# A gated mix of full and local attention: the local branch's sums by accumulating DMAs, padded weights loaded from DRAM

## The chip, the cores and the metric

The kernel runs on one core of a Trainium2 chip. A core has five engines with a queue of instructions each: TensorE (PE) multiplies matrices into the eight banks of PSUM, VectorE (DVE) and ScalarE (ACT) compute on SBUF and PSUM, GpSimd (POOL) and SyncE (SP) mostly issue DMAs here. Engines run side by side and wait for one another through semaphores. The metric is the device time of one execution in microseconds (us), as the median of the runs.

## The reference

Two attentions over 2048 positions of width 640, 32 heads of 20 each, mixed row by row by a sigmoid gate. Both take the input `x`; A attends to all positions, B to the eight positions p, p-2, ..., p-14.

```python
x = A_x
g = _sigmoid((x * gate_w).sum(-1, keepdims=True))
# A: q, k, v from x @ A_wqkv
p = _softmax(einsum("bhqd,bhkd->bhqk", q, k) * scale)
a = merge_heads(einsum("bhqk,bhkd->bhqd", p, v)) @ A_wo
# B: q, k, v from x @ B_wqkv; W, dil = 8, 2
idx = pos[:, None] - (arange(W) * dil)[None, :]
logits = where(idx >= 0, einsum("bhsd,bhswd->bhsw", q, kg) * scale, -1e9)
b = merge_heads(einsum("bhsw,bhswd->bhsd", softmax(logits), vg)) @ B_wo
return g * a + (1 - g) * b
```

`kg` and `vg` are the rows of k and v at the positions `idx`.

## The kernel before

**Branch A.** Queries go in 4 chunks of 512 positions (`qc`), heads in 8 quads of 4 (`q`): 32 groups. A group is 16 key blocks x 4 heads = 64 score matmuls of 32x128 by 32x512. They are cut into steps of 3 and 2 score banks, 819 steps in all. Each step is a set of score matmuls (L956), one exp on ACT over 3 or 2 banks (L969), and the PV matmuls (L977), which collect in one bank; a column of ones in `vA` gives the softmax sums. After a group the bank is transposed by VectorE into `rg` (L586), scaled by gate over sum and transposed back into `oTn` (L594 to L603). The next group's PV matmuls start over in the same bank and wait for L586.

The group's queries are projected just ahead: `cp_w` (L360) copies 80 weight columns from `WqkA` into a padded tile `WqP` with 32 columns a head (20 used, the first of them for a bound on the scores), five matmuls (L378) project, VectorE evacuates twice (`qtmp` L537, `qT` L545). In the first chunk the keys of each quad are made in the same way through `WkP` (`gen_k`). `WqkA` holds all q and k weights of branch A: two small loads for quad 0 at the start on ACT's queue, two of 700 KB on SP's.

**Branch B** runs beside it, one chunk of 512 positions at a time. Stage F (`gen_F`) projects q and k, multiplies them at the eight offsets (L739) and sums over the head with matmuls. Stage K (`gen_K`) projects v into `vB4`, makes the softmax over eight offsets, and for each of four blocks of 128 positions spreads the weights to `attnT` (eight PE transposes, one evacuation L830) and sums `vB4` x weight over the eight offsets on VectorE: the first product goes to `blkacc` (L847), each further one to `tmpB` (L853) and is added (L857), the last add goes to `oBacc` as bf16 (L863).

**Output.** `gen_fold` adds both branches' output projections per block and half width: 5 matmuls of B and 8 of A (13), evacuation, a store. For the last chunk `gen_prefold` does 5 of B and 6 of A (11) for eight pieces, 88 matmuls, and keeps them in `accin`; `last_fold`, behind the last exp, does the last two quads (16 matmuls, L665), adds (L672) and stores. The prefold needs stage K of the last chunk complete.

**The order** of each engine's queue is written out by a planner in Python when the program is built. It walks through the 819 steps, keeps a model clock for each engine, and lets "lanes" (generators such as `gen_F`, `gen_K`, `gen_fold`, the k, q and v projections) add instructions between the steps. A lane yields `("dve", need, weight)` or `("pe", need, weight)` and goes on when the model clock has room; `after(t)` holds it until task `t` is done by the model; a lane has a window of steps and goes on when it is behind its share. What a step needs and isn't there is forced (`force`), which takes no regard of room or waits. Lanes that are unfinished after step 819 are forced then, in order. The model charges each DMA 4000 ns from the moment at which its inputs are ready, and each engine instruction its `cost`. Banks 6 and 7 are handed to the lanes by `take` and `give`.

Dependencies come from keys: a task waits for the writers of what it reads, and for writers and readers of what it writes. A DMA's completion is always a semaphore wait, also between two DMAs of one queue. All engines take their queue in order. DMA semaphores rotate, 16 on SP and 12 on POOL.

Of the kernel before, what the change touches and what calls it, by code (L numbers as in the profile page):

```python
# [5 lines left out]
FP32 = mybir.dt.float32  # L6
# [3 lines left out]
ALU = mybir.AluOpType  # L10
# [208 lines left out]
def _build(ctx, nc, A_x, A_wqkv, A_wo, B_wqkv, B_wo, gate_w, out):  # L219
# [21 lines left out]
    bw = sb([P, 3328], BF16, "bw")  # L241
# [49 lines left out]
    lgt = [WqkA[:, 2 + i, D:D + 512] for i in range(2)]  # L291
    repp = [[WqkA[:, 0, D:D + 512], WqkA[:, 1, D:D + 512]], [WkP[i][:, 0:4, :].rearrange("p c k -> p (c k)") for i in range(2)]]
    rep_dead = [[("WkA", 1)], [("WkP", 0), ("WkP", 1)]]
    accin = WqkB[:, :, :].rearrange("p c k -> p (c k)").bitcast(FP32)[:, 0:4 * D].rearrange("p (b k) -> p b k", b=4)
    outl = WvB[:, :, :].rearrange("p c k -> p (c k)")[:, 0:4 * D].rearrange("p (b k) -> p b k", b=4)

# [7 lines left out]
        return bass.AP(tensor=t, offset=first.offset, ap=[[first.ap[0][0], P]] + dims)  # L304


    T("act", lambda e: e.dma_start(WqkA[:, :, D:D + 80], wA_v[:, :, D:D + 80]), writes=[("WkA", 0)], dma=True)
# [8 lines left out]

    T("act", sp_gw, writes=["gw"], dma=True)
    T("sp", lambda e: e.dma_start(WvA[:, :, 2:D + 2], wA_v[:, :, 2 * D:3 * D]), writes=["WvA"], dma=True)
    T("sp", lambda e: e.dma_start(WqkA[:, :, D + 80:2 * D], wA_v[:, :, D + 80:2 * D]), writes=[("WkA", 1)], dma=True)
    T("sp", lambda e: e.dma_start(WqkA[:, :, 80:D], wA_v[:, :, 80:D]), writes=[("WqA", 1)], dma=True)  # L320

    T("pool", lambda e: e.iota(itmp, [[1, P]], base=0, channel_multiplier=-1), writes=["itmp"])
    T("pool", lambda e: e.iota(stmp, [[P, CN], [-DH, 32]], base=0, channel_multiplier=1), writes=["stmp"])
# [16 lines left out]
        T("dve", lambda e, j=j: e.memset(e0[32 * j:32 * j + 1, :], 1.0), writes=["e0"])  # L340
        T("dve", lambda e, j=j: e.memset(nsel[32 * j:32 * j + 32, 32 * j:32 * j + 1], -1.0), writes=["nsel"])
    for i in range(2):
        T("dve", lambda e, i=i: e.memset(WkP[i][:, :, :], 0.0), writes=[("WkP", i)])
        T("dve", lambda e, i=i: e.memset(WqP[i][:, :, :], 0.0), writes=[("WqP", i)])
# [11 lines left out]

    def cp_w(dst, src_first):
        o_ap = fap(dst, dst[:, 0, 1:2], [[P, CN], [32, 4], [1, DH]])
        i_ap = fap(WqkA, src_first, [[2 * D, CN], [DH, 4], [1, DH]])
        return lambda e: e.tensor_copy(o_ap, i_ap)  # L360

    wk_made = set()

    def mk_wk(q):
        wk_made.add(q)
        return T("dve", cp_w(WkP[q % 2], WqkA[:, 0, D + 80 * q:D + 80 * q + 1]),
                 reads=[("WkA", 0 if q == 0 else 1)], writes=[("WkP", q % 2)], cost=370)

    def mk_wq(q, i):
        return T("dve", cp_w(WqP[i], WqkA[:, 0, 80 * q:80 * q + 1]),  # L370
                 reads=[("WqA", 0 if q == 0 else 1)], writes=[("WqP", i)], cost=370)

    def mm_part(b, mms, k0, n, reads, cost):

# [56 lines left out]
    def after(t):  # L431
        return ("t", t.fin)
# [88 lines left out]

    def gen_q(gi):
        qc, q = divmod(gi, NQUAD)
        i = gi % 2
        yield ("dve", 370.0, 0.0)
        yield after(mk_wq(q, i))
        while qc == 0 and not kl[q].done:
            yield ("poll",)
        b = yield from take()
        yield from chain(b, proj_mms(b, WqP[i], qc), [("WqP", i), "xT"])  # L530
# [155 lines left out]
    sm_b = fap(sm, sm[:, 0, 0:1], [[32, 4], [0, WIN], [1, 32]])  # L686
    prodctr = [0]
    fdone, ldone = {}, {}

    def gen_F(tc):  # L690

# [14 lines left out]
                yield ("dve", 690.0, 0.0)  # L706
                give(b, T("dve", lambda e, dst=dst, b=b: e.tensor_copy(dst, bank[b]), reads=[("bk", b)], writes=[key], cost=690))  # L707
        while tc > 0 and not ldone.get(tc - 1):
            yield ("poll",)
        while (NQUAD - 1) not in wk_made:  # L710
            yield ("poll",)
        for half in range(2):
            b = yield from take()
            slot = {}

            def sel(f, b=b, slot=slot):
                rs = [slot[(f, wp)] for wp in range(4)]

                def pe_l(e):
                    ins = None  # L720
                    for wp in range(4):
                        ins = e.matmul(bank[b][32 * wp:32 * wp + 32, :], Sel[:, f, :], prod[rs[wp]][:, :],  # L722
                                       start=(f == 0), stop=(f == CN - 1))
# [24 lines left out]
            yield ("dve", 690.0, 0.0)  # L748
            give(b, T("dve", lambda e, half=half, b=b: e.tensor_copy(lgt[half], bank[b]),
                      reads=[("bk", b)], writes=[("lgt", half), ("WkA", 1)], cost=690))  # L750
        if tc == 0:
            for w in range(1, WIN):
                row = 32 * (w % 4)
# [4 lines left out]
    def gen_K(tc):  # L758
# [77 lines left out]
        mk_aT(0, b)  # L836
        yield ("dve", 690.0, 690.0)
        give(b, ev_aT(0, b))
        for bl in range(4):
            ai = bl % 2  # L840
            for w in range(WIN):
                av = fap(bw, attnT[ai][:, w * P:w * P + 1], [[0, CN], [1, P]])
                off = PADB - DIL * w + bl * P
                vv = vB4[:, :, off:off + P]
                yield ("dve", 822.0, 822.0)
                if w == 0:
                    T("dve", lambda e, vv=vv, av=av: e.tensor_tensor(blkacc[:, :, :], vv, av, ALU.mult),  # L847
                      reads=[("aT", ai), "vB4"], writes=["blkacc"], cost=822)
# [4 lines left out]
                T("dve", lambda e, vv=vv, av=av: e.tensor_tensor(tmpB, vv, av, ALU.mult),  # L853
                  reads=[("aT", ai), "vB4"], writes=["tmpB"], cost=822)
                yield ("dve", 822.0, 822.0)
                if w < WIN - 1:
                    T("dve", lambda e: e.tensor_tensor(blkacc[:, :, :], blkacc[:, :, :], tmpB, ALU.add),  # L857
                      reads=["tmpB"], writes=["blkacc"], cost=822)
                else:
                    while tc >= 1 and not folddone.get(tc - 1):  # L860
                        yield ("poll",)
                    acc = oBacc[:, :, bl * P:(bl + 1) * P]
                    T("dve", lambda e, acc=acc: e.tensor_tensor(acc, blkacc[:, :, :], tmpB, ALU.add),  # L863
                      reads=["tmpB", "blkacc"], writes=[("oBacc", bl)], cost=822)
                if w == 3 and bl < 3:
                    yield after(tr)
                    b = yield from take()
# [8 lines left out]
    mk_wk(0)  # L876

    def pro_tr(t):
        bs = (0, 1, 2) if t % 2 == 0 else (3, 4, 5)
# [21 lines left out]

    def pro_k(t):
        b = 6 + t % 2
        mm_part(b, proj_mms(b, WkP[0], t), 0, CN, [("WkP", 0)] + [("xTt", t, k) for k in range(3)], 1100)
        k_evac(b, 0, t, "act")

    pro_tr(0)
    pro_tr(1)
    mk_wq(0, 0)
    pro_k(0)  # L910
    pro_tr(2)
    pro_k(1)
    consts_late()
    pro_tr(3)
    QB0 = 0
    mm_part(QB0, proj_mms(QB0, WqP[0], 0), 0, CN, [("WqP", 0)] + [("xTt", 0, k) for k in range(3)], 1100)
# [4 lines left out]
    pro_k(3)  # L921
    sch.bufs["xT"] = sch.bufs[("xTt", 3, 2)]
    mk_KM(0)
    for gi_ in range(2):
# [284 lines left out]
```

## Time and profile before

| | us |
|---|---|
| median of 2 runs | 1102.41 |
| the runs | 1106.39, 1098.44 |
| span of the profiled execution (its own full time is not among the runs) | 1091.2 |
| first exp starts, last exp ends | 27.8, 1080.3 |
| VectorE busy in the span | 579.7 |
| mean granted TensorE clock | 0.831 of full speed |

The span is the time from the first to the last instruction in one profiled execution. Further groups that the change touches, each with line, engine, operation, tiles, count, then busy us and mean ns of one:

```profile
L863 DVE TENSOR_TENSOR oBacc<-blkacc,bw 128x640 bf16<-128x640 f32 x16 | 13.2, 824 | 0.5
L360 DVE COPY WqP<-WqkA 128x400 bf16<-128x400 bf16 x32 | 11.6, 364 | 0.2 <-DMA WqkA<-in_A_wqkv_dram 0.2
L653 DVE COPY WqkB<-ps 128x320 f32<-128x320 f32 x8 | 3.9, 491 | 24.1 <-PE ps L378 24.1
```

The number behind the second bar is the engine's idle time just before these instructions, with what ended it. POOL is busy for 0.7 us in the whole span, and no DMA is issued from it.

### The profile page before, as it was taken

The page shows a single profiled execution, that of the slowest core. Times are in us where ns is not written, and L with a number is a line of the kernel's source. Part 1 is how long each engine was busy: PE and PEld are TensorE (multiplying, and loading weights), DVE is VectorE, ACT ScalarE, POOL GpSimd, SP SyncE. Part 2 cuts the span into 40 slices and gives each one's busy share as a digit, 9 for nine tenths or more (in the row PEclk, how much of TensorE's full clock was granted, in tenths as well). Part 3 has the DMA queues.
Part 4 walks back from the last instruction along what each step waited for, and adds up shares of the span by engine and source line. Part 5 has one row for each costly group of instructions (what it writes and reads, how often), then busy time and mean ns, then how long its engine had stood idle before and what let it go on. Part 6 is the DMA issues. An engine that isn't in the chain of part 4 may idle for free.

```text
span 1091.2 us, 15504 instructions
## 1 busy us (share of the span) xinstructions
PE 969.2 (89%) x5820; PEld 289.7 (27%) x5894; DVE 579.7 (53%) x1055; ACT 971.4 (89%) x842; POOL 0.7 (0%) x6
## 2 busy tenths in 40 slices
PE   6978899998798898989998988998888899799997
PEld 3323333322222222123332122233222223222231
DVE  4355434443635755762467767225787723777512
ACT  4868889988999988989999989999998989898996
POOL 0000000000000000000000000000000000000000
PEclk9879989998999756689998677999976699755695
DMA  8000000000000000000000000000000000000000
GB/s 277 1 1 15 17 1 2 1 23 9 1 2 1 1 1 1 1 1 7 7 7 7 1 1 1 7 8 7 7 2 1 1 7 13 7 1 1 1 1 25
DMA packets 11356, 12.79 MB, mean 12 GB/s; under 512 B 2708, under 2 KB 10644, under 8 KB 11284
## 3 DMA queue, kind: packets, MB, share of 16 engines
q1 hardware_dynamic: 9028, 11.27, 3.2%
q8 instruction: 49, 0.80, 0.3%
q10 hardware_dynamic: 2256, 0.53, 0.2%
q14 instruction: 23, 0.19, 0.1%
HBM read 9.18 MB, written 2.62 MB: 11 GB/s over the span
## 4 chain that ended last, share of the span: by engine, by line
PE 63%; ACT 21%; issue 9%; DVE 6%; DMA 1%; ACTq 0%; SPq 0%; DVEq 0%
ACT ebuf L969 21%; PE ps L956 20%; PE ps L378 19%; PE ps L977 19%; PE ps L453 2%; PE ps L543 1%; DVE bw L853 1%; PE ps L722 1%; DMA x_tm<-in_A_x_dram 1%; DVE blkacc L857 1%; PE ps L823 1%; DVE rg L586 1%; DVE qT L545 1%; DVE qtmp L537 0%; DVE WvB L672 0%
## 5 line engine op out<-in xcount | busy, mean ns | idle before, releaser
L969 ACT ACTIVATE ebuf<-ps 128x1536 bf16<-128x1536 f32 (+1 forms) x819 | 956.0, 1245 | 84.9 <-PE ps L956 64.3
L956 PE MATMUL ps<-qT,kT 32*128 32x512 bf16 x2048 | 372.9, 448 | 87.7 <-ACT ebuf L969 69.8
L977 PE MATMUL ps<-ebuf,vA 128*21 128x512 bf16 x2048 | 373.8, 452 | 3.3 <-DVE rg L586 1.2
L956 PEld LDWEIGHTS ps<-qT,kT 32*128 32x128 bf16 x2048 | 87.3, 93 | 370.5 <-PE ps L956 153.2
L977 PEld LDWEIGHTS ps<-ebuf,vA 128*21 128x21 bf16 x2048 | 77.7, 90 | 239.3 <-issue 229.7
L853 DVE TENSOR_TENSOR bw<-vB,bw 128x640 f32<-128x640 bf16 x112 | 91.9, 820 | 2.2
L857 DVE TENSOR_TENSOR blkacc<-blkacc,bw 128x640 f32<-128x640 f32 x96 | 79.0, 823 | 2.8
L739 DVE TENSOR_TENSOR prod<-qk 128x512 bf16<-128x512 bf16 x160 | 57.7, 418 | 22.3 <-PE ps L722 22.1
L707 DVE CAST qk<-ps 128x512 bf16<-128x512 f32 x40 | 27.6, 689 | 75.3 <-PE ps L378 72.6
L378 PE MATMUL ps<-xT,WqkB 128*128 128x512 bf16 x181 | 63.0, 413 | 3.2 <-issue 1.8
L537 DVE CAST qtmp<-ps 128x512 bf16<-128x512 f32 x32 | 22.1, 691 | 76.3 <-PE ps L378 73.6
L586 DVE STREAM_TRANSPOSE rg<-ps 128x512 f32<-128x512 f32 x32 | 22.9, 716 | 69.2 <-PE ps L977 69.2
L378 PE MATMUL ps<-xT,WqP 128*128 128x512 bf16 x134 | 52.1, 457 | 4.0 <-issue 1.8
L378 PE MATMUL ps<-woA_r,oTn 128*128 128x320 bf16 x240 | 54.2, 303 | 0.1
L390 DVE TENSOR_SCALAR kT<-ps,e 128x512 bf16<-128x512 f32 x28 | 20.9, 746 | 61.8 <-PE ps L378 60.0
L378 PE MATMUL ps<-xT,WkP 128*128 128x512 bf16 x145 | 48.8, 407 | 2.1 <-issue 1.0
L378 PE MATMUL ps<-WvA,oBacc 128*128 128x320 bf16 x160 | 38.0, 310 | 0.9 <-issue 0.4
L771 DVE CAST vB<-ps 128x512 bf16<-128x512 f32 x20 | 13.7, 687 | 46.5 <-PE ps L378 42.6
L633 DVE CAST outsb<-ps 128x320 bf16<-128x320 f32 x24 | 11.7, 488 | 44.7 <-PE ps L378 44.5
L545 DVE CAST qT<-ps 128x512 bf16<-128x512 f32 x32 | 22.1, 692 | 23.8 <-PE ps L543 22.6
L453 PE MATMUL ps<-WvA,xT 128*128 128x160 bf16 (+1 forms) x320 | 32.6, 244 | 1.5 <-DVE WvA L919 1.0
L378 PE MATMUL ps<-xT,WvB 128*128 128x512 bf16 x88 | 28.8, 389 | 0.8 <-DVE vB L771 0.4
(90 smaller groups left out, 448.4 us busy)
## 6 DMA issues: line engine op xcount, KB each, us to landing
x_tm<-in_A_x_dram SPq DMA_DIRECT2D x4, 640.0 KB
out_dram<-outsb SPq DMA_DIRECT2D x12, 160.0 KB
WqkB<-in_B_wqkv_dram SPq DMA_DIRECT2D x1, 1600.0 KB
WqkA<-in_A_wqkv_dram SPq DMA_DIRECT2D x2, 700.0 KB
WvA<-in_A_wqkv_dram SPq DMA_DIRECT2D x1, 800.0 KB
qk<-in_B_wqkv_dram SPq DMA_DIRECT2D x1, 800.0 KB
woA_r<-in_A_wo_dram SPq DMA_DIRECT2D x32, 25.0 KB
WvA<-in_B_wo_dram SPq DMA_DIRECT2D x5, 160.0 KB
```

The lines of the kernel that those rows point to most:

```text
L378: ins = e.matmul(o, l, r, start=(k0 + k == 0), stop=(k0 + k == n - 1))
L453: ins = e.matmul(bank[b][:, i_ * wn:(i_ + 1) * wn], xT[:, c, kb * P:(kb + 1) * P], WvA[:, c, w0:w0 + wn], start=(c == 0), stop=(c == CN - 1))
L537: T("dve", lambda e: e.tensor_copy(qtmp[:, :], bank[b]), reads=[("bk", b)], writes=["qtmp"], cost=690)
L545: return T("dve", lambda e: e.tensor_copy(qT[gi % NQT][:, :], bank[b]), reads=[("bk", b)], writes=[("qT", gi % NQT)], cost=690)
L586: return T("dve", lambda e: e.transpose(rg[i][:, :], bank[OB]), reads=[("ob", j) for j in range(4)], writes=[("rg", i)], cost=720)
L707: give(b, T("dve", lambda e, dst=dst, b=b: e.tensor_copy(dst, bank[b]), reads=[("bk", b)], writes=[key], cost=690))
L739: t = T("dve", lambda e, r=r, f=f, off=off: e.tensor_tensor(prod[r][:, :], qB[:, f, :], kB[:, f, off:off + 512], ALU.mult), reads=["qB", " ...
L853: T("dve", lambda e, vv=vv, av=av: e.tensor_tensor(tmpB, vv, av, ALU.mult), reads=[("aT", ai), "vB4"], writes=["tmpB"], cost=822)
L857: T("dve", lambda e: e.tensor_tensor(blkacc[:, :, :], blkacc[:, :, :], tmpB, ALU.add), reads=["tmpB"], writes=["blkacc"], cost=822)
L956: ins = e.matmul(bank[b0 + i], kT[32 * j:32 * j + 32, q, kb * P:(kb + 1) * P], qT[gi % NQT][32 * j:32 * j + 32, :], start=True, stop=True)
L969: return T("act", lambda e: e.activation(ebuf[s % NEB][:, 0:512 * n], ps[:, b0 * 512:(b0 + n) * 512], ACTF.Exp, scale=SCALE), reads=[("bk" ...
L977: ins = e.matmul(bank[OB][32 * j:32 * j + DH + 1, :], vA[:, q, kb, VW * j:VW * j + DH + 1], ebuf[s % NEB][:, i * 512:(i + 1) * 512], start ...
```

## The change

1. The running sum of a block of stage K. Products go as fp32 into a ring of three tiles `tmps`; for each, GpSimd's queue issues a DMA that adds the tile to `accs[ac]`, one of two accumulators that alternate by block. The first product of a block is written to `accs` directly. A block is closed by a copy from `accs` to `oBacc`, one block later (`close`). A product waits in the plan until the DMA that read its tile is done by the model.
2. `WqkA` shrinks to 160 columns, the weights of quad 0. All others are loaded by SP straight into `WkP` and `WqP`, five DMAs for a weight, one for each 128 rows, in runs of 20 elements; the weight of quad q+2 (or group gi+2) is issued when the projection with the tile's present content has been recorded. The copies L360 stay for quad 0 alone.
3. `lgt` and `repp`, which lay in dead columns of `WqkA`, get a tile of their own, `lgtr`; the wait of `gen_F` for the last `WkP` is gone.

```diff
-    tmpB = bw[:, 2048:2048 + 2 * D].bitcast(FP32).rearrange("p (c k) -> p c k", c=CN)
-    WqkA = sb([P, CN, 2 * D], BF16, "WqkA")
+    WqkA = sb([P, CN, 160], BF16, "WqkA")
+    lgtr = sb([P, 4, 512], BF16, "lgtr")
-    blkacc = sb([P, CN, P], FP32, "blkacc")
+    NTM = 3
+    tmps = [sb([P, D], FP32, "tmps%d" % i) for i in range(NTM)]
+    accs = [sb([P, D], FP32, "accs%d" % i) for i in range(2)]
...
-    T("sp", lambda e: e.dma_start(WqkA[:, :, D + 80:2 * D], wA_v[:, :, D + 80:2 * D]), writes=[("WkA", 1)], dma=True)
-    T("sp", lambda e: e.dma_start(WqkA[:, :, 80:D], wA_v[:, :, 80:D]), writes=[("WqA", 1)], dma=True)
...
+    def ld_w(dst, key, col):
+        for c in range(CN):
+            o_ap = fap(dst, dst[:, c, 1:2], [[32, 4], [1, DH]])
+            i_ap = bass.AP(tensor=A_wqkv.tensor, offset=A_wqkv.offset + c * P * 3 * D + col, ap=[[3 * D, P], [DH, 4], [1, DH]])
...
+            T("sp", fn, writes=[(key[0], key[1], c)], dma=True)
...
     def gen_k(q):
-        yield ("dve", 370.0, 0.0)
-        yield after(mk_wk(q))
         for tcc in range(4):
             b = yield from take()
-            yield from chain(b, proj_mms(b, WkP[q % 2], tcc), [("WkP", q % 2), "xT"])
+            yield from chain(b, proj_mms(b, WkP[q % 2], tcc), w_keys("WkP", q % 2) + ["xT"])
+            if tcc == 3 and q + 2 < NQUAD:
+                ld_wk(q + 2)
...
     def gen_q(gi):
-        yield ("dve", 370.0, 0.0)
-        yield after(mk_wq(q, i))
...
+        yield from chain(b, proj_mms(b, WqP[i], qc), w_keys("WqP", i) + ["xT"])
+        if gi + 2 < QCN * NQUAD:
+            ld_wq(gi + 2)
...
+        def close(bl):
+            ac, r, t = blkq.pop(0)[1:]
+            yield after(t)
+            yield ("dve", 822.0, 822.0)
+            while tc >= 1 and not folddone.get(tc - 1):
+                yield ("poll",)
+            acc = oBacc[:, :, bl * P:(bl + 1) * P]
+            T("dve", lambda e: e.tensor_copy(acc, acc3[ac]), reads=[("accs", ac)], writes=[("oBacc", bl)], cost=420)
...
-                T("dve", lambda e, vv=vv, av=av: e.tensor_tensor(tmpB, vv, av, ALU.mult),
-                  reads=[("aT", ai), "vB4"], writes=["tmpB"], cost=822)
-                yield ("dve", 822.0, 822.0)
...
+                r = tmctr[0] % NTM
+                tmctr[0] += 1
+                rd_ = tmrd.get(r)
+                if rd_ is not None:
+                    yield after(rd_)
+                    yield ("dve", 822.0, 0.0)
+                T("dve", lambda e, vv=vv, av=av, r=r: e.tensor_tensor(tmp3[r], vv, av, ALU.mult),
+                  reads=[("aT", ai), "vB4"], writes=[("tmps", r)], cost=822)
+                t = T("pool", lambda e, r=r, ac=ac: e.dma_start(accs[ac][:, :], tmps[r][:, :], accum_op=ALU.add),
+                      reads=[("tmps", r)], writes=[("accs", ac)], dma=True)
+                tmrd[r] = t
+                if w == 1 and blkq:
+                    yield from close(bl - 1)
+                if w == WIN - 1:
+                    blkq.append((bl, ac, r, t))
...
+        yield from close(3)
         bdone[tc] = True
```

More of the change, by code (lines that the diff above doesn't have):

```diff
@@ L240, in _build @@
     vB4 = sb([P, CN, 512 + PADB], BF16, "vB4")
-    bw = sb([P, 3328], BF16, "bw")
+    bw = sb([P, 2048], BF16, "bw")
     attnT = [bw[:, 1024 * i:1024 * i + 1024] for i in range(2)]
-    tmpB = bw[:, 2048:2048 + 2 * D].bitcast(FP32).rearrange("p (c k) -> p c k", c=CN)
     NPR = 6
@@ L288, in _build @@
     oBacc = sb([P, CN, 512], BF16, "oBacc")
-    blkacc = sb([P, CN, P], FP32, "blkacc")
-    lgt = [WqkA[:, 2 + i, D:D + 512] for i in range(2)]
-    repp = [[WqkA[:, 0, D:D + 512], WqkA[:, 1, D:D + 512]], [WkP[i][:, 0:4, :].rearrange("p c k -> p (c k)") for i in range(2)]]
-    rep_dead = [[("WkA", 1)], [("WkP", 0), ("WkP", 1)]]
+    NTM = 3
+    tmps = [sb([P, D], FP32, "tmps%d" % i) for i in range(NTM)]
+    accs = [sb([P, D], FP32, "accs%d" % i) for i in range(2)]
+    tmp3 = [t[:, :].rearrange("p (c k) -> p c k", c=CN) for t in tmps]
+    acc3 = [t[:, :].rearrange("p (c k) -> p c k", c=CN) for t in accs]
+    lgt = [lgtr[:, 2 + i, :] for i in range(2)]
+    repp = [[lgtr[:, 0, :], lgtr[:, 1, :]], [WkP[i][:, 0:4, :].rearrange("p c k -> p (c k)") for i in range(2)]]
+    rep_dead = [[], [("WkP", i, c) for i in range(2) for c in range(CN)]]
     accin = WqkB[:, :, :].rearrange("p c k -> p (c k)").bitcast(FP32)[:, 0:4 * D].rearrange("p (b k) -> p b k", b=4)
@@ L304, in fap @@
         return bass.AP(tensor=t, offset=first.offset, ap=[[first.ap[0][0], P]] + dims)
-    T("act", lambda e: e.dma_start(WqkA[:, :, D:D + 80], wA_v[:, :, D:D + 80]), writes=[("WkA", 0)], dma=True)
+    T("act", lambda e: e.dma_start(WqkA[:, :, 80:160], wA_v[:, :, D:D + 80]), writes=[("WkA", 0)], dma=True)
     for t in range(QCN):
@@ L342, in _build @@
     for i in range(2):
-        T("dve", lambda e, i=i: e.memset(WkP[i][:, :, :], 0.0), writes=[("WkP", i)])
-        T("dve", lambda e, i=i: e.memset(WqP[i][:, :, :], 0.0), writes=[("WqP", i)])
+        T("dve", lambda e, i=i: e.memset(WkP[i][:, :, :], 0.0), writes=[("WkP", i, c) for c in range(CN)])
+        T("dve", lambda e, i=i: e.memset(WqP[i][:, :, :], 0.0), writes=[("WqP", i, c) for c in range(CN)])
     def consts_late():
@@ L358, in cp_w, with mk_w0, fn, ld_wk @@
         o_ap = fap(dst, dst[:, 0, 1:2], [[P, CN], [32, 4], [1, DH]])
-        i_ap = fap(WqkA, src_first, [[2 * D, CN], [DH, 4], [1, DH]])
+        i_ap = fap(WqkA, src_first, [[160, CN], [DH, 4], [1, DH]])
         return lambda e: e.tensor_copy(o_ap, i_ap)
[L362 to L371, printed above, removed]
+    def mk_w0(dst, key, c0, src):
+        return T("dve", cp_w(dst, WqkA[:, 0, c0:c0 + 1]), reads=[src], writes=[key], cost=370)
+    def ld_w(dst, key, col):
+        for c in range(CN):
+            o_ap = fap(dst, dst[:, c, 1:2], [[32, 4], [1, DH]])
+            i_ap = bass.AP(tensor=A_wqkv.tensor, offset=A_wqkv.offset + c * P * 3 * D + col, ap=[[3 * D, P], [DH, 4], [1, DH]])
+            def fn(e, o_ap=o_ap, i_ap=i_ap):
+                with nc.allow_non_contiguous_dma(reason="runs of one head"):
+                    return e.dma_start(o_ap, i_ap)
+            T("sp", fn, writes=[(key[0], key[1], c)], dma=True)
+    def ld_wk(q):
+        ld_w(WkP[q % 2], ("WkP", q % 2), D + 80 * q)
+    def ld_wq(gi):
+        ld_w(WqP[gi % 2], ("WqP", gi % 2), 80 * (gi % NQUAD))
+    def w_keys(name, i):
+        return [(name, i, c) for c in range(CN)]
     def mm_part(b, mms, k0, n, reads, cost):
@@ L529, in gen_q @@
         b = yield from take()
-        yield from chain(b, proj_mms(b, WqP[i], qc), [("WqP", i), "xT"])
+        yield from chain(b, proj_mms(b, WqP[i], qc), w_keys("WqP", i) + ["xT"])
+        if gi + 2 < QCN * NQUAD:
+            ld_wq(gi + 2)
         yield ("dve", 690.0, 0.0)
@@ L688, in _build @@
     fdone, ldone = {}, {}
+    tmctr = [0]
+    tmrd = {}
     def gen_F(tc):
@@ L708, in gen_F @@
         while tc > 0 and not ldone.get(tc - 1):
-            yield ("poll",)
-        while (NQUAD - 1) not in wk_made:
             yield ("poll",)
@@ L749, in gen_F @@
             give(b, T("dve", lambda e, half=half, b=b: e.tensor_copy(lgt[half], bank[b]),
-                      reads=[("bk", b)], writes=[("lgt", half), ("WkA", 1)], cost=690))
+                      reads=[("bk", b)], writes=[("lgt", half)], cost=690))
         if tc == 0:
@@ L838, in gen_K @@
         give(b, ev_aT(0, b))
+        blkq = []
+        def close(bl):
[6 more added lines that the diff above has]
+            T("dve", lambda e: e.tensor_copy(acc, acc3[ac]), reads=[("accs", ac)], writes=[("oBacc", bl)], cost=420)
         for bl in range(4):
             ai = bl % 2
+            ac = bl % 2
             for w in range(WIN):
@@ L846, in gen_K @@
                 if w == 0:
-                    T("dve", lambda e, vv=vv, av=av: e.tensor_tensor(blkacc[:, :, :], vv, av, ALU.mult),
-                      reads=[("aT", ai), "vB4"], writes=["blkacc"], cost=822)
+                    T("dve", lambda e, vv=vv, av=av, ac=ac: e.tensor_tensor(acc3[ac], vv, av, ALU.mult),
+                      reads=[("aT", ai), "vB4"], writes=[("accs", ac)], cost=822)
                     if bl < 3:
@@ L852, in gen_K @@
                     continue
-                T("dve", lambda e, vv=vv, av=av: e.tensor_tensor(tmpB, vv, av, ALU.mult),
-                  reads=[("aT", ai), "vB4"], writes=["tmpB"], cost=822)
-                yield ("dve", 822.0, 822.0)
[L856 to L864, printed above, removed]
+                r = tmctr[0] % NTM
[13 more added lines that the diff above has]
+                    blkq.append((bl, ac, r, t))
                 if w == 3 and bl < 3:
@@ L872, in gen_K, with mk_k0, mk_q0 @@
                     give(b, ev_aT(bl + 1, b))
+        yield from close(3)
         bdone[tc] = True
-    mk_wk(0)
+    def mk_k0():
+        mk_w0(WkP[0], ("WkP", 0, 0), 80, ("WkA", 0))
+        for c in range(1, CN):
+            sch.bufs[("WkP", 0, c)] = [sch.bufs[("WkP", 0, 0)][0], []]
+    def mk_q0():
+        mk_w0(WqP[0], ("WqP", 0, 0), 0, ("WqA", 0))
+        for c in range(1, CN):
+            sch.bufs[("WqP", 0, c)] = [sch.bufs[("WqP", 0, 0)][0], []]
+    mk_k0()
     def pro_tr(t):
@@ L903, in pro_k @@
         b = 6 + t % 2
-        mm_part(b, proj_mms(b, WkP[0], t), 0, CN, [("WkP", 0)] + [("xTt", t, k) for k in range(3)], 1100)
+        mm_part(b, proj_mms(b, WkP[0], t), 0, CN, w_keys("WkP", 0) + [("xTt", t, k) for k in range(3)], 1100)
         k_evac(b, 0, t, "act")
@@ L908, in _build @@
     pro_tr(1)
-    mk_wq(0, 0)
+    mk_q0()
+    ld_wk(1)
+    ld_wq(1)
     pro_k(0)
@@ L915, in _build @@
     QB0 = 0
-    mm_part(QB0, proj_mms(QB0, WqP[0], 0), 0, CN, [("WqP", 0)] + [("xTt", 0, k) for k in range(3)], 1100)
+    mm_part(QB0, proj_mms(QB0, WqP[0], 0), 0, CN, w_keys("WqP", 0) + [("xTt", 0, k) for k in range(3)], 1100)
     pro_k(2)
@@ L921, in _build @@
     pro_k(3)
+    ld_wk(2)
+    ld_wq(2)
     sch.bufs["xT"] = sch.bufs[("xTt", 3, 2)]
```

## The prediction

> **What bounds the kernel now.** I read the page first: busy time, chain, groups.
>
> ```profile
> span 1091.2 us, 15504 instructions
> ...
> PE 969.2 (89%) x5820; PEld 289.7 (27%) x5894; DVE 579.7 (53%) x1055; ACT 971.4 (89%) x842; POOL 0.7 (0%) x6
> ...
> PE 63%; ACT 21%; issue 9%; DVE 6%; DMA 1%; ACTq 0%; SPq 0%; DVEq 0%
> ...
> L969 ACT ACTIVATE ebuf<-ps 128x1536 bf16<-128x1536 f32 (+1 forms) x819 | 956.0, 1245 | 84.9 <-PE ps L956 64.3
> ...
> L853 DVE TENSOR_TENSOR bw<-vB,bw 128x640 f32<-128x640 bf16 x112 | 91.9, 820 | 2.2
> L857 DVE TENSOR_TENSOR blkacc<-blkacc,bw 128x640 f32<-128x640 f32 x96 | 79.0, 823 | 2.8
> ```
>
> PE and ACT carry the kernel: 819 exps, 956.0 us of work in the 1052.5 us between the first exp (27.8 us) and the end of the last (1080.3). VectorE is on 6% of the chain. Its adds (L857) are the work the change takes off it, so I asked who waits for them:
>
> ```profile
> who waited for it (us, times):
>   PEld ps L378: 2.6, 5
>   PE ps L956: 0.5, 1
>   PEld ps L823: 0.4, 1
>   PE ps L378: 0.3, 1
> ```
>
> That is 3.8 us for 79.0 us of work; the same view gives 1.9 us for the products L853 and 1.8 us for the weight copies L360. So 7.5 us at most comes back directly. Then the stages at the end, busy us of PE, PEld, DVE, ACT, POOL, then the granted clock:
>
> ```profile
> 1022.00:1058.00 36.00, 35.18 (x232) 12.13 (x230) 9.19 (x18) 32.88 (x28) 0.00 (x0) 0.95 0.00 1
> 1058.00:1080.30 22.30, 19.66 (x102) 4.36 (x99) 0.49 (x1) 22.20 (x20) 0.00 (x0) 0.62 0.00 1
> 1080.30:1091.20 10.90, 4.22 (x19) 1.87 (x19) 6.29 (x13) 0.00 (x0) 0.00 (x0) 0.66 0.18 61
> ```
>
> In the first, the prefold of the last chunk (88 matmuls) runs under the exps; only 10.9 us lie behind the last exp. The change attacks exactly this.
>
> **What the change moves.** Removed from VectorE: 96 adds at 0.82 us (79.0), 16 closing adds (13.2) and 38 of 40 weight copies (0.36 each, 14). Added: 16 closing copies (between the 0.36 us of an L360 copy of 400 elements and the 0.82 of a closing add). The 112 adds become accumulating DMAs on GpSimd's queue. Each writes the accumulator that the previous one of its block wrote, so each waits for the previous landing; products go into a ring of three buffers, so product n waits, at the head of VectorE's in-order queue, for accumulate n-3. Behind it stand the evacuations of banks 6 and 7, the group's `rg` transpose (the next group's PV matmuls wait for it) and `qT`.
>
> The planner charges 4 us to a DMA and holds a product back until its buffer should be free. This stretches the local branch's stage K. In the changed program's recorded order, the steps (exps) from first to last accumulate are 253-350, 423-527 and 631-713 for chunks 0 to 2. Chunk 3 begins at step 777 of 819 and isn't done at the last step. What is left is written out behind the last exp: PE's order ends with the last block's 8 transposes, all 88 prefold matmuls and the 16 of the last fold; VectorE's has, behind the last group's norm, 13 more products, three `oBacc` copies, 8 prefold evacuations and 8 final adds. Cover for that work is gone.
>
> **Price of one accumulate (L).** The trace has no accumulating and no GpSimd DMA. The nearest rows are chains on SP's queue, each DMA waiting for the one before (total us, times, longest):
>
> ```profile
> SPq L570 <- DMA woA_r<-in_A_wo_dram: 29.3, 24, 1.3
> SPq L578 <- DMA WvA<-in_B_wo_dram: 14.7, 4, 3.7
> ```
>
> Waiting plus issue gives 1.2 + 0.3 = 1.5 us for a 25 KB load and 3.7 + 0.5 = 4.2 us for a 160 KB load in 128 rows of 1280 B. A final output store of 160 KB lands 1.8 us after issue. An accumulate moves 320 KB in 128 rows of 2560 B and has to read the destination too. Bounds: 1.8 us (faster than its bytes suggest) and 6.9 us (4.2 with the 2.7 us above the small load doubled for twice the bytes). I take 4.2, the nearest chained row of 128 rows. By the Trainium skill (DMA: Bandwidth & Descriptors, Anatomy of one DMA) a GpSimd DMA costs about 2.0 us plus bytes/436 GB/s, an estimate of 2.75 us here; the sum would be +46 us, 1148. No run here shows it yet; the 4.2 us row speaks for more.
>
> **The tail.** Accumulates of a block are serial; the first of a block can run beside the last of the block before. So four blocks take 7 + 6 + 6 + 6 = 25 L, at 4.2 us 105 us. From step 777 to the last exp are 42 steps; the last undisturbed stretch gives 1.167 us a step (29.2 us between the norms at 1051.8 and 1081.0, 25 steps), 49 us. So 105 - 49 = 56 us of chain lie behind the last exp. At small L the order sets a floor: about 4 us to the norm's end and the next product, then 12 L.
>
> Then come the closing copy (0.8) and the first prefold evacuation (0.5). Two of eight prefold pieces wait in their banks; the other 66 matmuls need banks back. The last fold shows their price at both clocks:
>
> ```profile
> 1080.85 2.32 PE L665 MATMUL ps<-woA_r,oTn 128*128 128x320 bf16 x8
> ...
> 1083.51 1.37 PE L665 MATMUL ps<-woA_r,oTn 128*128 128x320 bf16 x8 [0.34 <-DVE oTn L603]
> 1083.96 4.66 DVE L672 TENSOR_TENSOR WvB<-ps,WqkB 128x320 bf16<-128x320 f32 x8 [0.51 <-PE ps L665]
> ```
>
> 0.29 or 0.17 us each, 19 or 11 us; I take 15. Evacuations (0.49) hide beside them. The last fold's first eight: 1.8 (1.4 to 2.3). From its second eight to the end as now: 1091.2 - 1083.5 = 7.7. Sum behind the last exp: 56 + 0.8 + 0.5 + 15 + 1.8 + 7.7 = 82 us, where 10.9 stand now: **+71**.
>
> **The body.** Back come the 7.5 us of waits and, with the prefold gone from 1022-1058, 36.0 - 32.9 = 3.1 us down to ACT's busy time: -11. Against it stand the weights. SP now issues 190 loads of 20 KB in runs of 40 B for two of 700 KB, and branch B's weights (2.4 MB, 9 us at the 277 GB/s of the first slice) are queued behind the k weights of group 3, which wait for a projection at about step 22; their reader stands at step 32, some 13 us later. I take +5 us (0 to 10) for this and late weights. The ring costs nothing at 4.2 us: at 1.286 us a step ((1080.3 - 27.8)/819) the tightest places of chunk 2's order (product 7 at step 649, behind five serial accumulates: 18 x 1.286/5) stall only from L = 4.6 to 4.8 us on. Body -6; sum +71 - 6 = +65 on the profiled execution. Its own span is 1091.2; the median is 11.2 us longer for launch and spread between runs, which I carry over: 1102.4 + 65 = **1167**.
>
> **Rivals.**
> *The ring stalls the body* (L above 4.8). For: two reads and a write per byte, queue and descriptors on GpSimd. Against: planned spacing above 4.2. At L = 5.4: tail 135 - 49 = 86 of chain, 30 more than above; chunks need 135 us where they have 125, 134 and 105 (97, 104 and 82 steps): 10 + 1 + 30. Together 1167 + 71 = 1238. At 6.9 it is 1167 + 67 + 152 = 1386. Copies of VectorE that hold up accumulates would lead here, and the skill has such a rule (SBUF - State Buffer, SBUF: two separate sides): GpSimd can't write descriptors while VectorE runs a two-port copy. No row here shows it. Chance 0.28.
> *Short accumulates.* At 1.8 us: floor 4 + 21.6 = 26 of chain instead of 56, 1137; with body gains twice as large 1126. For: a 160 KB store lands in 1.8. Chance 0.09.
> *Faster: the body becomes ACT-bound.* Place: steps 253 to 777. All 96 us in which exps don't run would vanish because VectorE is 106 us freer: +71 - 96 = -25, 1077. It decides from a body gain of 93 us on; from 49 on it is no measurable change. For: DVE 0.6 busy in these stages. Against: 7.5 us of waits. Chance 0.03 with the cases between.
> *Weights late.* A 160 B-run load of 640 pieces took 6.8 us to land at the busy start; five loads of 512 pieces, if serial, are 34 us, more than a group of 29. If seven k groups each wait 5 to 10 us: +35 to +70, 1202 to 1237. Against: loads are queued without waiting for one another and one group ahead. Chance 0.05.
>
> **Numbers.** Forecast (L from 3 to 4.8: 1151 to 1182) 0.55; rivals 0.28, 0.09, 0.03, 0.05. Range 1142 to 1240: below it lie most of the short accumulates, 0.07, above it half of the ring's cases, 0.13. Two per cent (22 us) is about what a measurement here tells from no change. Faster 0.01; same 0.04, the short accumulates with more body gain and most of the ACT-bound cases; slower 0.95.
>
> **What would show it.** In the changed profile: a last exp near 1075, then 60 to 100 us with ACT empty; VectorE waiting for DMA at the products; accumulates about 4.2 us apart there; 66 matmuls in 11 to 19 us behind them. The ring rival shows `tmps` products waiting for DMA between 350 and 950 us with ACT idle; late weights show PE waiting for `WkP` or `WqP`. I am wrong if ACT is busy to the end, or if accumulates land in under 1.5 us.

## The result and the profile after

The changed kernel takes 1156.21 us (two runs, 1154.84 and 1157.59) against 1102.41: 1.049 times as long, with an interval of 1.043 to 1.056. That is +53.8 us between the medians, where +65 was forecast. The page of the changed kernel, with the rows that answer to those of before:

```profile
span 1152.9 us, 15953 instructions
...
PE 987.2 (86%) x5823; PEld 295.6 (26%) x5894; DVE 488.0 (42%) x921; ACT 971.2 (84%) x842; POOL 97.3 (8%) x118
...
q0 software_dynamic: 16128, 36.71, 17.2%
...
PE 59%; ACT 23%; issue 12%; DVE 4%; DMA 2%; POOL 1%; ACTq 0%; SPq 0%; DVEq 0%; POOLq 0%
...
L1013 ACT ACTIVATE ebuf<-ps 128x1536 bf16<-128x1536 f32 (+1 forms) x819 | 955.9, 1243 | 82.7 <-PE ps L1000 62.2
...
L887 POOL DMA_DIRECT2D accs<-tmps x112 | 96.7, 889 | 1030.3 <-DVE tmps L885 773.1
```

VectorE is busy 92 us less (579.7 to 488.0). ACT does the same 956 us of exps, and PE does the same matmuls (5820 and 5823 records, 969.2 and 987.2 us). So no work was added to the two engines that carry the kernel, and the span is still 61.7 us longer. The stages say where; again busy us of PE, PEld, VectorE, ACT and POOL, then the granted clock, for the last stretch before the end of the last exp (1077.9 us) and for what lies behind it:

```profile
1000.00:1077.90 77.90, 69.79 (x400) 19.26 (x400) 35.50 (x55) 74.69 (x65) 11.79 (x15) 0.72 0.31 60
1077.90:1152.90 75.00, 20.36 (x115) 12.38 (x115) 23.99 (x39) 0.01 (x1) 12.36 (x15) 0.61 0.37 74
```

Up to the last exp nothing is slower: ACT is busy for 74.7 of the 77.9 us, and the last exp ends 2.4 us earlier than before (1077.9 against 1080.3). Behind it ACT is empty for 75.0 us where 10.9 stood: +64.1 - 2.4 = +61.7, the whole of the difference. What fills the first 53 of these 75 us is the queue of GpSimd; its timeline there (start, us, instruction, idle time before and what ended it):

```profile
1083.39 0.86 POOL L887 DMA_DIRECT2D accs<-tmps  x1 [4.33 <-DVE tmps L885]
1087.19 0.86 POOL L887 DMA_DIRECT2D accs<-tmps  x1 [2.95 <-DMA accs<-tmps]
1090.99 0.86 POOL L887 DMA_DIRECT2D accs<-tmps  x1 [2.94 <-DMA accs<-tmps]
1094.78 0.86 POOL L887 DMA_DIRECT2D accs<-tmps  x1 [2.93 <-DMA accs<-tmps]
1098.56 0.86 POOL L887 DMA_DIRECT2D accs<-tmps  x1 [2.92 <-DMA accs<-tmps]
1102.36 1.75 POOL L887 DMA_DIRECT2D accs<-tmps  x2 [2.94 <-DMA accs<-tmps]
1107.99 0.86 POOL L887 DMA_DIRECT2D accs<-tmps  x1 [3.88 <-DMA accs<-tmps]
```

Each start is about 3.8 us after the last one: 0.86 to issue, 2.94 of waiting for the landing. That is L. At 1102.36 two go out together, the last of one block and the first of the next. The queue goes on like this to 1127.47, and that accumulate has landed at 1131.0, when VectorE and PE take over. The timeline of all engines at the two ends of the prefold:

```profile
1131.01 0.82 DVE L862 CAST oBacc<-accs 128x640 bf16<-128x640 f32 x1 [11.05 <-DMA accs<-tmps]
...
1132.37 1.49 PE L392 MATMUL ps<-WvA,oBacc 128*128 128x320 bf16 x5 [44.96 <-DVE WqkB L667]
...
1143.32 2.56 PE L679 MATMUL ps<-woA_r,oTn 128*128 128x320 bf16 x16
```

PE has stood idle for 45 us for one VectorE copy (L667) that frees a bank. This copy stands in VectorE's queue behind the closing copy of the last block (L862), and so behind all the accumulates. Then PE runs the 66 prefold matmuls in 1143.32 - 1132.37 = 10.95 us, and the last fold with its output takes the 9.6 us to the end.

The span grew by 61.7 us and the median by 53.8 because the profiled execution of before was near the short end: its span is 1091.2, while 54 later runs of the same kernel took 1092.2 to 1107.7, with medians of 1097.8, 1103.4 and 1098.3 on the three chips used below. Between span and time lie only 1.9 us (1152.9 and 1154.84).

### The profile page after: what moved, and what is told of

Its sections match the earlier page's. It is cut to its first block, busy times and chain, and to the rows that moved or that the text cites. A ratio compares the mean times of both kernels' runs of the same rounds, so it can differ in the third digit from the quotient of the medians.

```text
span 1152.9 us, 15953 instructions
## 1 busy us (share of the span) xinstructions
PE 987.2 (86%) x5823; PEld 295.6 (26%) x5894; DVE 488.0 (42%) x921; ACT 971.2 (84%) x842; POOL 97.3 (8%) x118
## 4 chain that ended last, share of the span: by engine, by line
PE 59%; ACT 23%; issue 12%; DVE 4%; DMA 2%; POOL 1%; ACTq 0%; SPq 0%; DVEq 0%; POOLq 0%
ACT ebuf L1013 22%; PE ps L1000 19%; PE ps L1021 18%; PE ps L392 17%; PE ps L467 2%; DMA accs<-tmps 1%; PE ps L837 1%; PE ps L736 1%; POOL accs L887 1%; DMA x_tm<-in_A_x_dram 1%; DVE rg L600 1%; PE ps L557 0%; DVE WvB L686 0%; DVE mx L806 0%; DVE L_sb L808 0%
## 5 line engine op out<-in xcount | busy, mean ns | idle before, releaser
L1013 ACT ACTIVATE ebuf<-ps 128x1536 bf16<-128x1536 f32 (+1 forms) x819 | 955.9, 1243 | 82.7 <-PE ps L1000 62.2
L1000 PE MATMUL ps<-qT,kT 32*128 32x512 bf16 x2048 | 381.4, 458 | 83.5 <-ACT ebuf L1013 66.5
L1021 PE MATMUL ps<-ebuf,vA 128*21 128x512 bf16 x2048 | 380.5, 461 | 4.3 <-DVE rg L600 2.0
L887 POOL DMA_DIRECT2D accs<-tmps x112 | 96.7, 889 | 1030.3 <-DVE tmps L885 773.1
L1000 PEld LDWEIGHTS ps<-qT,kT 32*128 32x128 bf16 x2048 | 87.7, 94 | 371.5 <-PE ps L1000 163.4
L885 DVE TENSOR_TENSOR tmps<-vB,bw 128x640 f32<-128x640 bf16 x112 | 89.2, 818 | 77.3 <-DMA accs<-tmps 77.1
L392 PE MATMUL ps<-xT,WqP 128*128 128x512 bf16 x135 | 55.0, 481 | 6.5 <-ACT ebuf L1013 3.0
L392 PE MATMUL ps<-xT,WqkB 128*128 128x512 bf16 x186 | 58.1, 390 | 1.4 <-issue 0.7
L392 PE MATMUL ps<-xT,WkP 128*128 128x512 bf16 x143 | 48.7, 416 | 1.7 <-ACT ebuf L1013 1.1
L392 PEld LDWEIGHTS ps<-WvA,oBacc 128*128 128x128 bf16 x160 | 13.8, 103 | 66.5 <-issue 58.6
```

The source lines that it names most:

```text
L392: ins = e.matmul(o, l, r, start=(k0 + k == 0), stop=(k0 + k == n - 1))
L885: T("dve", lambda e, vv=vv, av=av, r=r: e.tensor_tensor(tmp3[r], vv, av, ALU.mult), reads=[("aT", ai), "vB4"], writes=[("tmps", r)], cost=822)
L887: t = T("pool", lambda e, r=r, ac=ac: e.dma_start(accs[ac][:, :], tmps[r][:, :], accum_op=ALU.add), reads=[("tmps", r)], writes=[("accs", ...
L1000: ins = e.matmul(bank[b0 + i], kT[32 * j:32 * j + 32, q, kb * P:(kb + 1) * P], qT[gi % NQT][32 * j:32 * j + 32, :], start=True, stop=True)
L1013: return T("act", lambda e: e.activation(ebuf[s % NEB][:, 0:512 * n], ps[:, b0 * 512:(b0 + n) * 512], ACTF.Exp, scale=SCALE), reads=[("bk" ...
L1021: ins = e.matmul(bank[OB][32 * j:32 * j + DH + 1, :], vA[:, q, kb, VW * j:VW * j + DH + 1], ebuf[s % NEB][:, i * 512:(i + 1) * 512], start ...
```

## The experiments

Each group of runs has its own runs of the kernel before beside it, and ratios are against those. Times are medians, ratios are those of the means. The first four ran on one chip (before: 1097.78).

**Shorter accumulates.** `half_width` adds only half of each product, so the other half of every sum's accumulations is left out. It asks whether the tail is 25 chained accumulates.

```diff
-                t = T("pool", lambda e, r=r, ac=ac: e.dma_start(accs[ac][:, :], tmps[r][:, :], accum_op=ALU.add),
+                t = T("pool", lambda e, r=r, ac=ac: e.dma_start(accs[ac][:, 0:320], tmps[r][:, 0:320], accum_op=ALU.add),
```

> Each accumulate moves columns 0 to 319 of 640 (the other half of the sums keeps only its first product: left out). The order of every engine is unchanged, so only the price L of one accumulate changes. Serial-chain theory: the chain behind the last exp shrinks by 25 times the change in L. If the 16 engines' data time (about 1.8 of 3.8 us by packet times) halves, L falls to about 2.9 us and the time by about 22 us, to some 1134. If L is almost all fixed (the Trainium skill's 2.0 us + bytes/436 GB/s, page DMA: Bandwidth & Descriptors, gives -0.38 us), some 1147. Rival, the tail is set by something else than the accumulates (bank hand-over, prefold): no change, 1156.

It took 1143.92 us, 1.043 times before (1.038 to 1.047). That lies between the two times named in advance (1134 and 1147). The span fell by 10.1 us, from 1152.9 to 1142.8, where 25 times the fall in L (3.79 to 3.03) is 19. GpSimd's timeline in this kernel shows what caught the rest:

```profile
1067.29 0.86 POOL L887 DMA_DIRECT2D accs<-tmps  x1 [2.20 <-DMA accs<-tmps]
1070.32 1.75 POOL L887 DMA_DIRECT2D accs<-tmps  x2 [2.17 <-DMA accs<-tmps]
1082.81 0.86 POOL L887 DMA_DIRECT2D accs<-tmps  x1 [10.74 <-DVE tmps L885]
1085.87 0.86 POOL L887 DMA_DIRECT2D accs<-tmps  x1 [2.20 <-DMA accs<-tmps]
```

The chain ran ahead and then stood still for 10.74 us, waiting for a product. VectorE's timeline tells why the product was late:

```profile
1067.03 0.83 DVE L885 TENSOR_TENSOR tmps<-vB,bw 128x640 f32<-128x640 bf16 x1 [0.89 <-DMA accs<-tmps]
1078.05 0.72 DVE L600 STREAM_TRANSPOSE rg<-ps 128x512 f32<-128x512 f32 x1 [10.19 <-PE ps L1021]
...
1081.15 2.28 DVE L885 TENSOR_TENSOR tmps<-vB,bw 128x640 f32<-128x640 bf16 x3
```

In VectorE's order the next product stands behind the last group's norm, whose first step needs the last PV matmul, and that needs the last exp. So 12 serial accumulates always start behind the last exp, however short they are. This is the floor of the prediction, and it binds at both widths. From the last exp to the first accumulate behind the norm it is 5.5 us in both (1077.9 to 1083.39; 1077.3 to 1082.81). From there to the last landing it is 47.6 and 38.6 us, that is 12 L plus 2.2 us in both (12 x 3.78 = 45.4; 12 x 3.03 = 36.4), most of it the longer step at the block edge (5.63 and 4.86 us instead of L). Only 12 of the 25 shorter accumulates could be seen in the time.

**Chunk 3's sums on VectorE.** `chunk3_adds_on_vector` keeps all else of the change.

```diff
+                if tc == 3:
+                    yield ("dve", 822.0, 822.0)
+                    t = T("dve", lambda e, r=r, ac=ac: e.tensor_tensor(accs[ac][:, :], accs[ac][:, :], tmps[r][:, :], ALU.add),
+                          reads=[("tmps", r)], writes=[("accs", ac)], cost=822)
+                else:
                     t = T("pool", lambda e, r=r, ac=ac: e.dma_start(accs[ac][:, :], tmps[r][:, :], accum_op=ALU.add),
```

> Chunks 0 to 2 as changed, chunk 3's adds on VectorE again, planned at 0.82 us each. Tail theory: 12 products and adds (10.3 us), a closing copy (0.8), then prefold and last fold uncovered as now (0.6 + 11 + 9.6) stand behind the last norm (3.2): some 36 us behind the last exp instead of 75, so 39 us less than the changed kernel, some 1117. Rival, the body is what got slower: about 1156 still.

It took 1118.77 us, 1.019 times before (1.014 to 1.024), +21.0, as expected. In its timeline the prefold's matmuls start 38 us earlier than in the changed kernel:

```profile
1094.02 1.49 PE L392 MATMUL ps<-WvA,oBacc 128*128 128x320 bf16 x5 [9.26 <-DVE WqkB L667]
```

So the chain of accumulates of one chunk is worth some 38 of the 64 us behind the last exp, shown by taking it away. What stays is that stage K still ends there: in this kernel's order, too, the last products and the prefold come behind the last group's norm, most likely because the plan charges chunks 0 to 2 their accumulates as before; no run tried that alone.

**A planned price below the real one.** `plan_charge_3us` changes the planner alone.

```diff
-            t.fin = max(self.clk[stream], ready) + 4000.0
+            t.fin = max(self.clk[stream], ready) + (3000.0 if stream == "pool" else 4000.0)
```

> The planner charges 3.0 instead of 4.0 us for an accumulate; nothing else is edited. In the recorded order chunk 3's stage K and the prefold then end before the last step. Theory (the 4 us charge pushed chunk 3 past the last exp): the tail is back at about 11 us. The real price of 3.8 us is above the planned spacing in chunk 3 alone (64 steps, some 82 us, for 25 x 3.78 = 95), so VectorE stalls there by up to 12 us, partly felt: 1093 to 1115. Rival, accumulates in the body stall VectorE and all others as soon as they are denser (the ring): 1130 or more.

It took 1124.64 us, 1.024 times before (1.020 to 1.029), +26.9: above what was expected. The tail is gone, as expected: the last exp ends at 1115.2 and 11.9 us follow. But now the body is late. At the ends of the four chunks, the last group's norm ends 2.7, 11.5, 24.9 and 34.9 us later than in the profiled execution of before. (This profile is the slowest of four runs and that of before near the short end, so the last figure is above the 26.9 us of the medians.) The view of waits of this kernel (total us, times, longest):

```profile
DVE tmps L885 <- DMA accs<-tmps: 85.2, 36, 4.0
ACT ebuf L1013 <- PE ps L1000: 84.1, 119, 4.6
...
ACT ebuf L1013 <- PE ps L1021: 25.6, 16, 6.9
...
PE ps L1021 <- DVE rg L600: 12.5, 6, 6.4
```

And the same view of the changed kernel:

```profile
DVE tmps L885 <- DMA accs<-tmps: 77.1, 31, 3.0
...
ACT ebuf L1013 <- PE ps L1000: 62.2, 108, 2.8
...
ACT ebuf L1013 <- PE ps L1021: 14.4, 17, 1.4
...
PE ps L1021 <- DVE rg L600: 2.0, 8, 0.6
```

The total of VectorE's wait at the products hardly differs (85.2 and 77.1). What differs is who stands behind it: here PE's PV matmuls wait up to 6.4 us for the `rg` transpose, ACT up to 6.9 us for them, and ACT's waits for score matmuls (L1000) grow from 62.2 to 84.1 us. This is the ring rival, brought about by the plan instead of by L. The ring stalls the body where real L is above the planned spacing: the prediction's threshold of 4.6 to 4.8 us at a charge of 4, scaled to a charge of 3, is 3.45 to 3.6 (an estimate), and L is 3.78. About 25 x 0.3 = 7 us a chunk follow from that, near the 9 a chunk seen on average. How much of the lateness is a lower granted clock (0.800 to 0.821 in these four runs, 0.819 to 0.831 in before beside them) was not separated.

**Half the chain length.** `two_chains` sends products alternately to the two accumulators and closes a block with one VectorE add, so each accumulate waits for the one before the last.

```diff
-            T("dve", lambda e: e.tensor_copy(acc, acc3[ac]), reads=[("accs", ac)], writes=[("oBacc", bl)], cost=420)
+            T("dve", lambda e: e.tensor_tensor(acc, acc3[0], acc3[1], ALU.add), reads=[("accs", 0), ("accs", 1)],
+              writes=[("oBacc", bl)], cost=822)
...
-                if w == 0:
+                ac = w % 2
+                if w < 2:
```

> Even offsets accumulate into one tile and odd ones into the other, a block closes with one add of both: three serial accumulates in each of two chains, none across blocks (24 a chunk instead of 28). In the recorded order stage K and the prefold end before the last step. Serial-latency theory: two accumulates in flight land in little more time than one; the tail is about 11 us and the time 1095 to 1110. Rival, the accumulates are limited by throughput (two in flight take turns): pairs are 7 to 8 us apart, VectorE stalls in every chunk, 1120 or more.

It took 1106.43 us, 1.0075 times before (1.0035 to 1.0114): 45 of the 54 us come back, with accumulates of the same size (96 of them, since two products of a block go straight into an accumulator). They land 3.5 us after issue in the median (5.7 at most), although two are mostly in flight, so they do not take turns. The last exp ends at 1095.4 and 11.9 us follow, so the tail is as short as in before and what is left of the loss lies in the body.

The next three ran on a second chip (before: 1103.37).

**The weights alone.** `weights_only` has parts 2 and 3 of the change and stage K as before.

```diff
-    WqkA = sb([P, CN, 2 * D], BF16, "WqkA")
+    WqkA = sb([P, CN, 160], BF16, "WqkA")
+    lgtr = sb([P, 4, 512], BF16, "lgtr")
...
-        yield after(mk_wk(q))
+            if tcc == 3 and q + 2 < NQUAD:
+                ld_wk(q + 2)
```

> Stage K's sums on VectorE as before; only the weights come straight from DRAM. Theory: the 38 copies saved 1.8 us of waits and the loads arrive in time, so between 4 us faster and 4 us slower than before. Rival, weights late: PE waits for WkP or WqP, 10 to 35 us slower.

It took 1101.2 us, 0.997 times before (0.995 to 0.9995).

**The adds alone.** `no_adds` is the kernel before with 96 of its 112 VectorE adds left out, so all but the closing step of each sum is missing.

```diff
-                yield ("dve", 822.0, 822.0)
-                if w < WIN - 1:
-                    T("dve", lambda e: e.tensor_tensor(blkacc[:, :, :], blkacc[:, :, :], tmpB, ALU.add),
-                      reads=["tmpB"], writes=["blkacc"], cost=822)
-                else:
+                if w == WIN - 1:
+                    yield ("dve", 822.0, 822.0)
```

> The kernel before without 96 of its 112 adds (left out: only the first and the last product of each sum remain), with nothing in their place: the most that any place for the adds could bring. Theory (VectorE isn't what the kernel waits for): the waits on the adds, 3.8 us, and little more come back: 0 to 10 us faster than before. Rival, VectorE-bound stages: 30 us or more faster.

It took 1099.8 us, 0.998 times before (0.994 to 1.0015). Its profile page has VectorE at 501.5 us where before has 579.7:

```profile
PE 984.9 (89%) x5822; PEld 292.0 (26%) x5894; DVE 501.5 (45%) x959; ACT 972.4 (88%) x842; POOL 0.7 (0%) x6
```

Seventy-eight us of VectorE's work taken away, with nothing put in their place, give no gain that clears the noise. No form of this offload could have gained what the adds' busy time suggests. The interval does allow the 3.8 us of waits to have come back, and the mean granted clock of the runs speaks for some gain: the four runs of `no_adds` at 0.812 to 0.816 took 1097.8 to 1104.3 us, the six runs of before beside it at 0.813 to 0.816 took 1105.8 to 1107.7. At a like clock the kernel without the adds is about 6 us shorter in the mean, but its clock was lower (median of the fast runs 0.8155, before 0.820). Whether leaving out the adds lowers the clock, no run shows.

**Two chains with a dearer plan.** `two_chains_charge_4p5us` asks whether the rest of `two_chains`' loss is a plan a little too tight.

```diff
-            t.fin = max(self.clk[stream], ready) + 4000.0
+            t.fin = max(self.clk[stream], ready) + (4500.0 if stream == "pool" else 4000.0)
```

> As two_chains, with 4.5 instead of 4.0 us charged for an accumulate, so that products are planned further apart; stage K and the prefold still end before the last step. Theory (what is left of the loss of two_chains, 8 us, are stalls at the ring): fewer stalls, 0 to 5 us slower than before. Rival, the loss is another (weights, contention): 8 us slower still.

It took 1110.33 us, 1.0066 times before (1.0042 to 1.009), as `two_chains` did. So the rival (8 us slower still) held: the dearer plan does not take the loss away.

The last two ran on a third chip (before: 1098.26).

**The traffic without the waits.** `idle_accumulates` is `weights_only` with 96 accumulates of full size into tiles that nobody reads.

```diff
-                    T("dve", lambda e: e.tensor_tensor(blkacc[:, :, :], blkacc[:, :, :], tmpB, ALU.add),
+                    ta = T("dve", lambda e: e.tensor_tensor(blkacc[:, :, :], blkacc[:, :, :], tmpB, ALU.add),
+                    T("pool", lambda e, i=w % 2: e.dma_start(scr[i][:, :], src0[:, :], accum_op=ALU.add),
+                      reads=["src0"], writes=[("scr", w % 2)], dma=True, extra=(ta,))
```

> weights_only plus 96 accumulating DMAs of 320 KB, one issued behind each add of VectorE, from a tile of constants into two tiles of their own (even and odd offsets) that no engine reads: the traffic of two_chains without its waits. If what two_chains still loses against before (7 to 8 us) is traffic or the queue (contention with PE, ACT or VectorE), this kernel is 7 to 10 us slower than weights_only. If it is waits for the accumulates, the two are equal within 3 us.

It took 1101.17 us, 1.0019 times before (0.9988 to 1.005).

**The weights again.** `weights_only_2` is the kernel of `weights_only` with no further edit, on the same chip as `idle_accumulates`.

> The same kernel as weights_only, beside idle_accumulates on one chip: 0.995 to 1.000 of before.

It took 1101.67 us, 1.0031 times before (1.0002 to 1.006). That is above what was expected. On one chip the weights part is 0.3% faster, on the other 0.3% slower: it is worth nothing that these runs can settle. Against it, the 96 idle accumulates cost -0.5 us, nothing that these runs can tell, where 7 to 10 us were expected if traffic or the queue were the cause. The groups of `idle_accumulates` show that VectorE's adds beside them last as long as in before, 823 ns:

```profile
L873 DVE TENSOR_TENSOR blkacc<-blkacc,bw 128x640 f32<-128x640 f32 x96 | 79.0, 823 | 2.7
```

So neither the accumulates' traffic, nor their issue, nor the small runs of the weights slow anything that these runs can tell. The cost of the changed kernel is its chain of waits, and where the plan puts the work around it.

The 7 to 9 us of the two-chain versions are another matter. They go together with a lower mean granted clock. `two_chains` had 0.810 to 0.821 where before beside it had 0.819 to 0.831; its runs at 0.818 and 0.821 took 1103.6 and 1104.0 us, and the run of before at 0.819 took 1104.6. `two_chains_charge_4p5us` had 0.804 to 0.810, lower than any of the 24 runs of before beside it (0.813 to 0.840). `idle_accumulates` had 0.813 to 0.832, much as before beside it (0.819 to 0.834). So at a like clock, as far as the runs overlap, `two_chains` is no slower than before. Whether the waits for the accumulates lower the clock, or something else does, stays open: no run varied the clock alone.

## Why the prediction was right, and where it was off

The prediction has the right sign, place and mechanism, and its range holds the time. By its own steps:

- **The order: right.** Chunk 3 was forecast to begin 49 us before the last exp ends and to be unfinished there. Its first accumulate is issued at 1029.20, 48.7 us before. This came from the recorded order and a planner's charge of 4 us, not from the chip's price of a DMA.
- **L, taken as 4.2: mis-sized.** It is 3.78 chained, so the nearest row (the chained 160 KB load) was 11% too high. The two widths split L into about 2.3 us that do not depend on size and 0.76 us for each 160 KB. By the Trainium skill (DMA: Bandwidth & Descriptors, Anatomy of one DMA) the estimate was 2.75, and the sum by it 1148. The trace does not agree: landing alone is 3.5 us after issue. The Trainium skill's fixed part of 2.0 us is near the 2.3; its rate of 436 GB/s makes 0.38 us for 160 KB, half of the 0.76.
- **The chain behind the last exp, 25 L - 49 = 56: measured 53.1, by the other branch.** At 3.78 this formula gives 45.5, and the floor (4 + 12 L = 49.4) is the larger. The floor was named only for small L. But 4 + 12 L is the larger below L = 53/13 = 4.1 us. `half_width` shows it. Its 4 us were 5.5, and 2.2 us, mostly at the block edge, were not in it: 5.5 + 45.4 + 2.2 = 53.1. Two errors, L and the branch, nearly cancelled, so part of the agreement is luck.
- **66 matmuls, 15 us: mis-sized.** They took 10.95, or 0.166 each, the faster of the two rates that the prediction quoted. The copy (0.75), the evacuation (0.6) and the last fold to the end (9.6 against 9.5) are as forecast. Behind the last exp 75.0 against 82.
- **Body, -6: not settled.** Between the two profiled executions it was -2.4. Between the medians it is 53.8 - 64.1 = -10.3, if the tail is the same in every run. Runs of before alone spread from 1092.2 to 1107.7 us, so these runs can't tell -6 from either. `no_adds` bounds one term: with the adds gone the mean falls by 0.2%, and at most by 0.6% (6 us) by its interval, so their 3.8 us of waits may have come back, and the 79 us of their busy time did not.
- **The carry-over, 11.2 us for launch and spread: wrong in its naming.** Launch is about 2 us; the rest was the profiled execution's place in the spread. Of the 11 us by which the forecast is too high, 3.3 come from the sum (65 against 61.7) and 7.9 from this term: between the changed kernel's profiled span and its median lie 3.3 us (1152.9 and 1156.21), not 11.2.
- **The rivals.** The ring rival (0.28) is a real mechanism and did not come, because L stayed below the planned spacing: the norms of all 32 groups end within -4.8 to +3.1 us of before. Short accumulates fell with L = 3.78. The ACT-bound body fell with `no_adds`. Late weights fell with `weights_only`: PE waited for a weight tile 0.4 us at most.
- **The rule on copies of VectorE** (the Trainium skill, SBUF — State Buffer, SBUF: two separate sides) by which GpSimd can't write descriptors beside a two-port copy: no sign of it here. Issue took 859 ns at the least and in the median (1212 at the most), landing 3.5 us at the least and in the median. Of the 112, 26 landed later, 4.0 to 5.9 us after issue; the slowest two that were alone in the queue (5.57 us at 714.74, 5.25 us at 912.02) had no VectorE instruction beside them. No run shows in which mode VectorE's copies ran, nor what made the 26 late.

## What to carry to other kernels

Ask who waits for the engine before taking work off it: here 79 us of adds were waited for 3.8 us, and leaving them out altogether gained nothing that clears the noise. Compare runs at a like granted clock before explaining a difference of a few us: here a lower clock hid some 6 us of gain in one kernel (`no_adds`) and went with the loss of another (`two_chains`). A chain of DMAs into one accumulator costs its latency times its length, and where a planner knows that price it will spread the work to fit, until the work falls out of the end of the kernel; read the recorded order for what stands behind the last unit of the engine that carries it. A planned price below the real one only trades the tail for stalls in the body (1.024 here); a shorter dependence, with two accumulators, gave most of the loss back (1.0075).

## What the runs showed of the hardware

- An accumulating DMA of 320 KB from SBUF to SBUF in 128 rows: 0.86 us to issue on GpSimd, landed 3.5 us after, 3.78 us from one to the next in a chain; at 160 KB 2.8 and 3.03.
- Of 112, 26 landed 4.0 to 5.9 us after issue; the slowest was the second of two issued back to back.
- With two mostly in flight (`two_chains`), the median landing stays at 3.5 us.
- 96 of them beside the whole kernel (31 MB) slow nothing that these runs can tell: 1101.17 against 1101.67 us.
- Loading weights in runs of 40 B (`weights_only`) makes 102,996 packets under 512 B where there were 2,708, and takes the queue's share of the 16 engines from 3.2% to 8.8%. With one group's lead it was hidden.
- The time of one kernel goes with the mean granted clock: on one chip the kernel before took 1105.8 to 1107.7 us in six runs at 0.813 to 0.816, and 1097.9 to 1102.1 in five at 0.824 and 0.825.
